# Batch 0's value products in one float32 part instead of three float32r parts

## The chip, the core and the metric

The kernel runs on one core of a Trainium2 chip. The core has a matrix engine (PE, with its weight loads listed as PEld), a vector engine (DVE), a scalar engine (ACT), a general engine (POOL) and a queue engine that sends DMAs (SP). The metric is device time in microseconds (us) from one execution; less is better.

## The reference

Three layers, one after the other, on 4 batches of 576 positions. The middle one is the place of the change.

```python
# 1. attention with a window of 32 (heads 0-3) or a dilated window (heads 4-7), 8 heads of 64
x = attn(q, k, v)                       # (4, 576, 512)
# 2. channel mix, w_r 512x512, w_k 512x1024, w_v 1024x512
xk = mu_k * x + (1 - mu_k) * x_prev
xr = mu_r * x + (1 - mu_r) * x_prev
k = np.maximum(xk @ w_k, 0.0)
v = k * k @ w_v
r = 1 / (1 + np.exp(-(xr @ w_r)))
x = r * v
# 3. gate to 2 of 4 experts, each a causal attention of width 64
```

## The kernel before

The work is laid out with features on partitions: a tile of activations is 128 features by 288 positions (half a batch, called a chunk, c = 0 or 1), and a product takes a 128x128 block of weights and streams the 288 columns past it. To come near float32 with the fast format float32r, `product` splits both factors in a rounded part and a rest (`hi`, `lo`) and adds three products of parts: hi by hi, hi weights by lo data, lo weights by hi data. So each pair of blocks costs three matmuls.

For the channel mix of a batch `b` (`dbatch`), PE makes per chunk `z` (4 outputs of `w_r`, function `receptance`), `h` (8 outputs of `w_k`, `keys`) and `v` (4 outputs of `w_v`, each over 8 blocks, `values_of`). Behind each `h` ACT takes the relu (`r`), then the square is halved and split in `kh` and `kl`; for batch 0 this is done with ACT and DVE passes over 128x288. Names such as `h_1_6` in the order below are chunk and output; `v_0_1` is chunk 0, output 1 of batch 0.

The weights come as 64-bit numbers. `load` brings a raw piece by DMA, `conv` makes float32 of it (`split_cols`: an ACT pass L679, two DVE passes L681 and L682) and splits it (ACT copy L687 to `w*_hi`, DVE subtraction L688 to `w*_lo`), each over 128x1024. The four pieces of `w_v` use the staging tiles `raw` and `vw` of the attention, and one in `x1`, so the first loads of batch 1's attention (`rqk`, L176, and `vw`, L204) wait until a piece is let go.

The attention of batch b+1 runs beside the channel mix of batch b. For a pair of heads (`sc_0` to `sc_3` are batch 1's pairs) q and k are loaded, turned by DVE (`qT`, `kT`; L276, for the dilated pairs 2 and 3 L271), PE makes scores (`sc`, L318), DVE masks them (L337), ACT takes exponents (L342), DVE scales (L354), PE turns the weights (`pt`, L382), ACT copies them (`pts`, L383), and PE multiplies by v (`av`, L394). A program-wide table of steps (`when`) says behind which step of `dbatch` a load or a `conv` is written, and the two streams are merged by `goal`. Within this a scheduler decides the order on each engine before the run; on the chip each engine then takes its instructions strictly in that order, so one that waits holds all behind it. The matmuls of attention are on plain float32 tiles.

Of the kernel before, what the change touches and what calls it, by code (L numbers as in the profile page):

```python
# [21 lines left out]
def tile_dilated_attention__rwkv_channel_mix__moe_attention(  # L22
# [131 lines left out]
    def load_qk(ap, dp, b, hp):  # L154

        dil = hp >= NP // 2
        qk = []
        if b == 0:  # L160
            if hp % 2 == 0:
                early["raw"] = dp.tile([128, 8, 512], F32R, tag=("wv_hi", "wv_lo")[hp // 2], name=f"rqk_{hp}",
                                       bufs=1).bitcast(F32).rearrange("p k f -> p (k f)")
# [343 lines left out]
    def mix_feature(n, c, w, f, b=0):  # L507

        t0 = CH * c
        x = X[b][:, f, 1 + t0 : 1 + t0 + CH]  # L510
        xp = X[b][:, f, t0 : t0 + CH]
        m, hi, lo = (a[:, f, :] for a in mixing[n])
        nc.scalar.activation(m, xp, AF.Copy, scale=mus[:, 1, w, f : f + 1])  # L513
        nc.vector.scalar_tensor_tensor(out=m, in0=x, scalar=mus[:, 0, w, f : f + 1], in1=m, op0=ALU.mult, op1=ALU.add)  # L514
        if b == 0:
            nc.scalar.copy(hi, m)
            nc.vector.tensor_sub(lo, m, hi.bitcast(F32))  # L517

# [45 lines left out]
    def keys(dp, b, c, fo, kh, kl, xk, wts):  # L564
# [10 lines left out]
        nc.vector.scalar_tensor_tensor(out=r, in0=r, scalar=0.5, in1=p if b else r, op0=ALU.mult, op1=ALU.mult)  # L575
# [11 lines left out]
    def dbatch(dp, dq, b, xr, wts, nxt):  # L587

        z, xk = [], []
        for c in range(2):  # L590
            z.append((dp if c else dq).tile([128, KT, CH], F32, tag=f"z{c}", name=f"z_{b}_{c}", bufs=1))
            for fo in range(KT):
                receptance(dp, b, c, fo, z[c], xr[c], wts)
# [3 lines left out]
        if b == 0:  # L597

            k2 = [(dp.tile(shape, F32R, tag="kh", name="kh_0_0", bufs=1), dp.tile(shape, F32R, tag="kl", name="kl_0_0", bufs=1)),
                  (xpool.tile(shape, F32R, tag="x3", name="kh_0_1", bufs=1), xpool.tile(shape, F32R, tag="x2", name="kl_0_1", bufs=1))]  # L600
# [13 lines left out]
        for c in range(2):  # L614
            k2 = (dp.tile(shape, F32R, tag="kh", name=f"kh_{b}_{c}", bufs=1), dp.tile(shape, F32R, tag="kl", name=f"kl_{b}_{c}", bufs=1))
            for fo in range(FT):
                keys(dp, b, c, fo, *k2, xk[c], wts)
# [3 lines left out]
            for fo in range(KT):  # L621
                values_of(b, c, fo, z[c], k2, wts)
# [38 lines left out]
    with tc.tile_pool(name="apool", bufs=2, side="left") as ap:  # L661
# [12 lines left out]
        def split_cols(raw, hi, lo, i):  # L674
# [7 lines left out]
            nc.vector.scalar_tensor_tensor(out=low, in0=high, scalar=3, in1=low,  # L682
                                           op0=ALU.logical_shift_left, op1=ALU.bitwise_or)
            w = low.bitcast(F32)
            cols = raw.shape[2]
            part_hi, part_lo = hi[:, :, i * cols : (i + 1) * cols], lo[:, :, i * cols : (i + 1) * cols]
            nc.scalar.copy(part_hi, w)  # L687
            marks["split"] = nc.vector.tensor_sub(part_lo, w, part_hi.bitcast(F32)).ins  # L688
# [4 lines left out]
        def load(x, i):  # L693
            pool, src, kts, cols = specs[x]
            if x not in wts:
                wts[x] = tuple(pool.tile([128, kts, cols], F32R, tag=f"w{x}_{h}", name=f"w{x}_{h}") for h in ("hi", "lo"))
            raws[x, i] = load_cols(src, kts, i, {"r": "hl", "k": "3RV1", "v": "RV1V"}[x][i])

        def conv(x, i):
            split_cols(raws.pop((x, i)), *wts[x], i)  # L700
            marks[f"split {x}{i}"] = marks["split"]


        when = {}
        for what, step in {"Lk1": 1, "r0": 18, "Lk2": 18, "r1": 22, "k0": 24, "Lk3": 24, "k1": 24, "Lv0": 24, "k2": 26,
# [20 lines left out]
        def mixed(b):  # L726
            yield from dbatch(dp, dq, b, mixes[b], wts, nxt(b))
# [8 lines left out]
        mixes[0] = [mixing[n][1:] for n in range(2)]  # L736
# [511 lines left out]
```

## Time and profile before

| | us |
|---|---|
| three runs | 548.56, 548.83, 549.34 |
| median | 548.83 |
| span of the profiled execution | 547.2 |

The profile is of one execution and shows its span, from the first to the last instruction; 1.6 us of the median lie around it. A row of a group of instructions has the line, the engine, the operation, its output and inputs by the program's names, shapes, the count, total busy us and mean ns of one, then the idle time ahead and what ended it. A matmul's record lasts longer than the distance to the next one, since matmuls are pipelined: its rate is read from the distance between starts.

### The profile page before, as it was taken

What the parts mean: (1) busy time and instruction counts of PE and PEld (TensorE: products, weight loads), DVE (VectorE), ACT (ScalarE), POOL (GpSimd) and SP (SyncE); (2) the same over time, 40 slices, a digit from 0 to 9 for tenths busy, and PEclk for the clock granted to TensorE, in tenths of its full rate; (3) what the DMA queues carried; (4) which work ended last, traced back from release to release, by engine and by line L of the source; (5) the groups of instructions that cost most, each with busy time, mean ns of one, the idle gap of its engine ahead of it and who ended that gap; (6) DMA issues with size and microseconds to landing.
All of it is one profiled execution on the core that took longest, in us unless ns stands there. A gap on an engine that the chain in (4) does not pass through costs nothing.

```text
span 547.2 us, 12500 instructions
## 1 busy us (share of the span) xinstructions
PE 525.8 (96%) x4653; PEld 476.1 (87%) x4657; DVE 350.8 (64%) x1153; ACT 336.4 (61%) x959; POOL 65.6 (12%) x99
## 2 busy tenths in 40 slices
PE   8987997999999999999999999999999999999996
PEld 4657996889999999999999999999977988988763
DVE  3788989695767588375451516448686559566752
ACT  2789978675884484663544526137576657656862
POOL 8500000010342031221022212000000000000000
PEclk9997999999999999999999999999999999999999
DMA  9959376876545663130100410055504705425313
GB/s 166 237 171 295 107 202 148 145 133 133 110 105 132 142 141 87 37 96 34 34 1 1 106 51 1 1 131 121 141 20 111 201 8 131 103 67 121 108 39 97
DMA packets 130173, 57.66 MB, mean 105 GB/s; under 512 B 109928, under 2 KB 117184, under 8 KB 130112
## 3 DMA queue, kind: packets, MB, share of 16 engines
q1 hardware_dynamic: 129392, 55.88, 43.2%
q8 instruction: 37, 0.61, 0.5%
q0 software_dynamic: 416, 0.44, 0.4%
q10 hardware_dynamic: 304, 0.53, 0.3%
q14 instruction: 24, 0.20, 0.1%
HBM read 34.42 MB, written 10.03 MB: 81 GB/s over the span
## 4 chain that ended last, share of the span: by engine, by line
PE 73%; DVE 9%; ACT 7%; SPq 4%; DMA 3%; issue 2%; POOL 1%; DVEq 0%; ACTq 0%; POOLq 0%
PE v L539 16%; PE h L539 11%; PE z L539 5%; PE av L1062 5%; PE pv L888 5%; PE po L1148 5%; PE pt L1025 4%; PE pq L539 4%; PE pk L539 4%; PE av L394 2%; PE sc L974 2%; PE sc L976 2%; SPq L189 2%; PE idle L76 2%; ACT pe L342 1%
## 5 line engine op out<-in xcount | busy, mean ns | idle before, releaser
L539 PE MATMUL h<-xh,wk_hi 128*128 128x288 f32 x256 | 76.3, 300 | 1.3 <-ACT r L568 0.8
L539 PE MATMUL v<-kh,wv_hi 128*128 128x288 f32 x256 | 74.9, 299 | 2.5 <-ACT r L568 1.9
L539 PE MATMUL h<-xl,wk_hi 128*128 128x288 f32 x256 | 75.5, 295 | 0.3 <-DVE xl L517 0.3
L539 PE MATMUL h<-xh,wk_lo 128*128 128x288 f32 x256 | 75.3, 294 | 0.4 <-DVE wk_lo L688 0.4
L539 PE MATMUL v<-kh,wv_lo 128*128 128x288 f32 x256 | 74.7, 296 | 0.0
L539 PE MATMUL v<-kl,wv_hi 128*128 128x288 f32 x256 | 74.7, 297 | 0.0
L986 ACT ACTIVATE pe<-pe,st 128x64 f32<-128x64 f32 (+4 forms) x80 | 44.8, 561 | 16.2 <-DVE st L980 15.8
L514 DVE SCALAR_TENSOR_TENSOR m<-x,mus,m 128x288 f32<-128x288 f32 x64 | 30.4, 512 | 34.5 <-ACT m L513 34.5
L529 POOL TENSOR_TENSOR xl<-m,xh 128x576 fp32r<-128x576 f32 x24 | 35.3, 1484 | 129.6 <-ACT xh L528 97.1
L539 PEld LDWEIGHTS v<-kh,wv_hi 128*128 128x128 f32 x256 | 47.6, 188 | 3.5 <-ACT r L568 2.3
L539 PEld LDWEIGHTS h<-xh,wk_hi 128*128 128x128 f32 x256 | 47.8, 187 | 2.7 <-ACT r L568 1.3
L539 PEld LDWEIGHTS h<-xh,wk_lo 128*128 128x128 f32 x256 | 48.2, 188 | 0.7 <-DVE wk_lo L688 0.7
L539 PEld LDWEIGHTS h<-xl,wk_hi 128*128 128x128 f32 x256 | 48.1, 188 | 0.5 <-DVE xl L517 0.5
L539 PEld LDWEIGHTS v<-kh,wv_lo 128*128 128x128 f32 x256 | 47.8, 188 | 0.4
L539 PEld LDWEIGHTS v<-kl,wv_hi 128*128 128x128 f32 x256 | 47.7, 188 | 0.4
L342 ACT ACTIVATE pe<-pe,st 128x96 f32<-128x96 f32 x108 | 39.0, 363 | 13.1 <-DVE st L337 13.1
L568 ACT ACTIVATE r<-h 128x288 f32<-128x288 f32 x64 | 25.8, 410 | 34.0 <-PE h L539 28.2
L980 DVE CUSTOM_DVE_ANT_0 pe<-sc,cmask 128x64 f32<-128x64 f32 (+4 forms) x80 | 33.1, 426 | 17.4 <-PE sc L976 17.0
L578 DVE TENSOR_TENSOR kl<-r,kh 128x288 fp32r<-128x288 f32 x50 | 31.1, 627 | 16.5 <-ACT kh L576 16.2
L539 PE MATMUL z<-xl,wr_hi 128*128 128x288 f32 x128 | 38.8, 304 | 0.1
L539 PE MATMUL z<-xh,wr_hi 128*128 128x288 f32 x128 | 38.8, 308 | 0.0
L539 PE MATMUL z<-xh,wr_lo 128*128 128x288 f32 x128 | 37.9, 299 | 0.0
(197 smaller groups left out, 1388.6 us busy)
## 6 DMA issues: line engine op xcount, KB each, us to landing
kk<-kh SPq DMA_DIRECT2D x32, 144.0 KB, 2.7
kl<-kl SPq DMA_DIRECT2D x32, 144.0 KB, 2.8
raw_in_moe_w_k_dram<-in_moe_w_k_dram SPq DMA_DIRECT2D x4, 1024.0 KB, 8.6
raw_in_moe_w_v_dram<-in_moe_w_v_dram SPq DMA_DIRECT2D x4, 1024.0 KB, 6.0
out_dram<-ob SPq DMA_DIRECT2D x14, 256.0 KB, 2.5
rqk<-in_q_dram SPq DMA_DIRECT2D x48, 72.0 KB, 2.6
rqk<-in_k_dram SPq DMA_DIRECT2D x48, 72.0 KB, 2.7
moved<-turned SPq DMA_DIRECT2D x8, 432.0 KB, 3.1
```

The source lines that it names most:

```text
L342: nc.scalar.activation(pe[:, t, :], pe[:, t, :] if b else sc[:, c0 : c0 + WK], AF.Exp, bias=st[:, 0, t : t + 1], scale=-1.0, accum_out=st[ ...
L514: nc.vector.scalar_tensor_tensor(out=m, in0=x, scalar=mus[:, 0, w, f : f + 1], in1=m, op0=ALU.mult, op1=ALU.add)
L529: nc.gpsimd.tensor_sub(lo[:, f], m[:, f], hi[:, f].bitcast(F32))
L539: marks["product"] = nc.tensor.matmul(o, w[:, kt, wsl], x[:, kt, :], start=(n == 0), stop=(n == last)).ins
L568: nc.scalar.activation(r, p, AF.Relu)
L578: half.tensor_sub(kl[:, fo, :], r, kh[:, fo, :].bitcast(F32))
L888: nc.tensor.matmul(p, x[:, kt, t0 : t0 + tn], w[:, kt, 512:772], start=(n == 0), stop=(n == 3 * KT - 1))
L980: nc.vector.tensor_tensor_reduce(out=pe[:tn, PO[t] + c0 : PO[t] + c1], in0=sc, in1=m, scale=-0.125, scalar=(BIG if i == 0 else st[:tn, 1, ...
L986: nc.scalar.activation(pb, pb, AF.Exp, bias=st[:tn, 0, t : t + 1], scale=-1.0, accum_out=st[:tn, 2, t : t + 1])
L1025: marks[f"turn {b}{e}"] = nc.tensor.transpose(pt[:kn, c0 : c0 + 128], pe[:, PO[t] + k0 : PO[t] + k0 + kn], ident).ins
L1062: ins = nc.tensor.matmul(av1[p0 : p0 + 64, q0 - 64 : q1 - 64], vh[kb][:kn], w[:kn, c0 : c0 + q1 - q0], start=(kb == blocks[0]), stop=(kb = ...
L1148: nc.tensor.matmul(sums[t], x[:, t0 : t0 + 128], w[:, h, :], start=(h == 0 and n == 0), stop=(h == 1 and n == 2))
```

## The change

The value products of batch 0, and no others, are made of whole float32 tiles: one matmul for each block of weights, with the halved square `k_0` as it is and the weights as they were put together. In detail:

- `conv` writes a piece of `w_v` out of its raw tile into a tile of its own (`wv_whole`, the fourth into `spare`); splitting it is a step of its own, `finish`, written at steps 66 to 72, after the value products of batch 0. `w_r` and `w_k` are finished in `conv`, as before, with their `lo` part in four tiles instead of one.
- In batch 0 `keys` writes one tile per chunk: for three outputs of four DVE multiplies the relu by the product in PSUM, and for every fourth ACT squares and halves it. There are no `kh` and `kl`.
- The first raw q and k of pairs 2 and 3 of batch 0 lie in the tile `wk_hi` instead of `wv_lo`.

```diff
     def keys(dp, b, c, fo, k2, xk):
         p = ps(bank(b), f"h_{b}_{c}_{fo}")[:, :CH]
-        product(p, wts["k"], xk, range(KT), slice(128 * fo, 128 * fo + 128))
+        weighted(p, b, "k", xk, fo)
         r = dp.tile([128, CH], F32, tag="r", name=f"r_{b}_{c}_{fo}", bufs=2)
         nc.scalar.activation(r, p, AF.Relu)
-        if b == 0 and 2 <= fo < 6:
-            nc.scalar.activation(r, r, AF.Square)
-            nc.scalar.activation(kh[:, fo, :], r, AF.Copy, scale=0.5)
-            nc.vector.scalar_tensor_tensor(out=kl[:, fo, :], in0=r, scalar=0.5, in1=kh[:, fo, :].bitcast(F32),
-                                           op0=ALU.mult, op1=ALU.subtract)
+        kh = k2[0]
+        if b == 0:
+            if fo % 4 == 3:
+                nc.scalar.activation(r, r, AF.Square)
+                nc.scalar.activation(kh[:, fo, :], r, AF.Copy, scale=0.5)
+            else:
+                nc.vector.scalar_tensor_tensor(out=kh[:, fo, :], in0=r, scalar=0.5, in1=p, op0=ALU.mult, op1=ALU.mult)
             return
...
+    def weighted(o, b, x, xs, fo):
+        cols = 1024 // (FT if x == "v" else KT)
+        i, at = divmod(128 * fo, cols)
+        wsl = slice(at, at + 128)
+        kts = range(KT if x != "v" else FT)
+        if b or x not in WHOLE:
+            product(o, (wts[x, "hi"][i], wts[x, "lo"][i]), xs, kts, wsl)
+            return
+        for kt in kts:
+            marks["product"] = nc.tensor.matmul(o, wts[x, "whole"][i][:, kt, wsl], xs[0][:, kt, :], start=(kt == 0),
+                                                stop=(kt == kts[-1])).ins
...
+        def finish(x, i):
...
+            nc.scalar.copy(hi, w)
+            marks[f"split {x}{i}"] = nc.vector.tensor_sub(lo, w, hi.bitcast(F32)).ins
+        WHOLE = "v"
```

The change moves instructions. On PE, the rows behind the scores of pair 1 are, before (`kh_0` and `kl_0` are the parts of chunk 0, `kh_1` and `kl_1` those of chunk 1):

```order
L382 MATMUL pt_0_0_1349<-ident,pe_0_1285 96x128 x3
L382 MATMUL pt_0_1_1380<-ident,pe_0_1285 96x128 x3
L539 MATMUL v_1_0_1624<-kl_1_1016,wv_hi 128x288
L539 MATMUL v_1_0_1624<-kh_1_1015,wv_lo 128x288
L539 MATMUL v_0_1_1703<-kh_0_1013,wv_hi 128x288
L539 MATMUL v_0_1_1703<-kl_0_1014,wv_hi 128x288
L539 MATMUL v_0_1_1703<-kh_0_1013,wv_lo 128x288
```

and in the changed kernel, from the first value product on:

```order
L557 MATMUL v_0_0_1487<-k_0_0_1015,wv_whole_1033 128x288 x8
L557 MATMUL v_1_0_1576<-k_0_1_1016,wv_whole_1033 128x288 x6
L318 MATMUL sc_1_5_1414<-kT_1_1409,qT_1_1407 64x96 x2
L318 MATMUL sc_1_0_1413<-kT_1_1409,qT_1_1407 64x96 x2
L318 MATMUL sc_1_5_1414<-kT_1_1409,qT_1_1407 64x96 x2
L318 MATMUL sc_1_0_1413<-kT_1_1409,qT_1_1407 64x96 x2
L382 MATMUL pt_0_0_1322<-ident,pe_0_1259 96x128 x3
L382 MATMUL pt_0_1_1351<-ident,pe_0_1259 96x128 x3
```

An output that took 24 rows takes 8, and the twelve of `h_1_7`, which stood ahead of `sc_0`, now stand between `sc_0` and `v_0_0`. Behind these rows stand four matmuls of `v_0_1`, the products `av_0_0`, a `pt`, the twelve of `h_1_6` and then the scores `sc_2`.

On DVE, where the last pieces of `w_k` and the first of `w_v` are converted (`raw_in_moe_w_k_dram_671` before and `_669` after is the piece for outputs 4 and 5), the rows before are:

```order
L688 TENSOR_TENSOR wk_lo<-raw_in_moe_w_k_dram_821,wk_hi 128x4x256
L517 TENSOR_TENSOR xl_1_3_996<-m_1_3_994,xh_1_3_995 128x288
L575 SCALAR_TENSOR_TENSOR r_0_1_1055<-r_0_1_1055 128x288
L688 TENSOR_TENSOR wk_lo<-raw_in_moe_w_k_dram_671,wk_hi 128x4x256
L517 TENSOR_TENSOR xl_1_3_996<-m_1_3_994,xh_1_3_995 128x288 x3
L578 TENSOR_TENSOR kl_0_1014<-r_0_0_1030,kh_0_1013 128x288
L681 TENSOR_SCALAR raw_in_moe_w_v_dram_845<-raw_in_moe_w_v_dram_845 128x1024
L578 TENSOR_TENSOR kl_0_1014<-r_0_1_1055,kh_0_1013 128x288
L682 SCALAR_TENSOR_TENSOR raw_in_moe_w_v_dram_845<-raw_in_moe_w_v_dram_845 128x1024
L572 SCALAR_TENSOR_TENSOR kl_0_1014<-r_0_2_1073,kh_0_1013 128x288
L575 SCALAR_TENSOR_TENSOR r_1_0_1091<-r_1_0_1091 128x288
L688 TENSOR_TENSOR wv_lo<-raw_in_moe_w_v_dram_845,wv_hi 128x8x128
```

and after:

```order
L748 TENSOR_TENSOR wk_lo_963<-raw_in_moe_w_k_dram_822,wk_hi 128x1024
L521 TENSOR_TENSOR xl_1_3_998<-m_1_3_996,xh_1_3_997 128x288
L593 SCALAR_TENSOR_TENSOR k_0_0_1015<-r_0_1_1052,h_0_1_1039 128x288
L701 TENSOR_SCALAR raw_in_moe_w_v_dram_845<-raw_in_moe_w_v_dram_845 128x1024
L748 TENSOR_TENSOR wk_lo_879<-raw_in_moe_w_k_dram_669,wk_hi 128x1024
L521 TENSOR_TENSOR xl_1_3_998<-m_1_3_996,xh_1_3_997 128x288 x3
L593 SCALAR_TENSOR_TENSOR k_0_0_1015<-r_0_2_1068,h_0_2_1055 128x288
L702 SCALAR_TENSOR_TENSOR wv_whole_1033<-raw_in_moe_w_v_dram_845 128x1024
L748 TENSOR_TENSOR wv_lo_1944<-wv_whole_1033,wv_hi 128x1024
L593 SCALAR_TENSOR_TENSOR k_0_1_1016<-r_1_0_1084,h_1_0_1071 128x288
```

The `kl` rows are gone, and the first pass over the first piece of `w_v` (L701) now stands ahead of the `wk_lo` of outputs 4 and 5. The split of that first piece still stands here although it is written at step 66; those of the other three pieces stand some 95, 130 and 160 rows further on, and the four copies to `wv_hi` stay in this stretch of ACT's order.

Also on DVE, the turning of pair 2's q (`qT_2`) stands before the change behind all the work on pair 1:

```order
L352 TENSOR_SCALAR st_1_1443<-st_1_1443 128x5
L353 RECIPROCAL st_1_1443<-st_1_1443 128x5
L354 TENSOR_TENSOR pe_1_1442<-pe_1_1442,st_1_1443 128x480
L271 STREAM_TRANSPOSE qT_2_1585<-rqk 128x144x4
L514 SCALAR_TENSOR_TENSOR m_0_4_1872<-x_1255,mus,m_0_4_1872 128x288
L271 STREAM_TRANSPOSE kT_2_1587<-rqk 128x144x4
```

and after it, ahead of the first look at pair 1's scores:

```order
L353 RECIPROCAL st_0_1260<-st_0_1260 128x5
L605 SCALAR_TENSOR_TENSOR x_212<-z_0_847,v_0_0_1487 128x288
L354 TENSOR_TENSOR pe_0_1259<-pe_0_1259,st_0_1260 128x480
L271 STREAM_TRANSPOSE qT_2_1537<-rqk 128x144x4
L337 ISA pe_1_1411,st_1_1412<-sc_1_5_1414,m_next 128x96
```

So `qT_2` moved ahead by the nine masked readings of `sc_1` and the scaling of `pe_1`.

## Rows read from the trace of the kernel before

**Rows 1.** The page: engines' shares of the chain that ended last.

```profile
PE 73%; DVE 9%; ACT 7%; SPq 4%; DMA 3%; issue 2%; POOL 1%; DVEq 0%; ACTq 0%; POOLq 0%
```

**Rows 2.** Stretches (from:to, length), busy us of PE, PEld, DVE, ACT, POOL; PE clock; DMA.

```profile
90.00:100.00 10.00, 7.82 (x84) 7.20 (x85) 9.97 (x55) 9.95 (x45) 0.00 (x0) 1.00 0.63 119
120.00:130.00 10.00, 10.00 (x129) 8.83 (x128) 7.89 (x36) 7.65 (x32) 0.00 (x0) 1.00 0.70 122
```

**Rows 3.** Waits of PE from 60 to 145 us: total us, times, longest.

```profile
PE v L539 <- ACT r L568: 1.9, 2, 1.2
PE sc L318 <- DVE kT L276: 0.9, 1, 0.9
PE h L539 <- ACT r L568: 0.8, 2, 0.5
PE sc L318 <- DVE kT L271: 0.7, 1, 0.7
PE pt L382 <- DVE pe L354: 0.7, 2, 0.5
PE h L539 <- DVE wk_lo L688: 0.4, 1, 0.4
PE h L539 <- DVE xl L517: 0.3, 1, 0.3
```

**Rows 4.** Timeline of PE around the first value product: start, duration, idle ahead.

```profile
87.37 0.29 PE L539 MATMUL h<-xh,wk_lo 128*128 128x288 f32 x1
87.81 1.06 PE L318 MATMUL sc<-kT,qT 64*64 64x96 f32 x36
90.04 0.40 PE L539 MATMUL v<-kh,wv_hi 128*128 128x288 f32 x1 [1.18 <-ACT r L568]
90.27 0.29 PE L539 MATMUL v<-kl,wv_hi 128*128 128x288 f32 x1
```

**Rows 5.** Pieces of the chain that ended last: start, length, what.

```profile
122.00 0.71 PE av L394 x20
...
275.02 12.77 PE v L539 x96
...
388.44 0.77 PE pt L1025 x7
```

**Rows 6.** Timeline of PEld in a float32 product of two experts, 512 then 384 columns.

```profile
400.57 0.20 PEld L1062 LDWEIGHTS av<-wt,vt 128*64 128x64 f32 x4
401.06 0.14 PEld L1062 LDWEIGHTS av<-wt,vt 128*64 128x64 f32 x2 [0.29 <-issue]
401.48 0.14 PEld L1062 LDWEIGHTS av<-wt,vt 128*64 128x64 f32 x2 [0.29 <-issue]
```

**Rows 7.** Groups of PE from 60 to 145 us: one of batch 0's three.

```profile
L539 PE MATMUL v<-kh,wv_hi 128*128 128x288 f32 x64 | 19.3, 304 | 1.9 <-ACT r L568 1.9
```

**Rows 8.** Groups of DVE from 58 to 142 us.

```profile
L688 DVE TENSOR_TENSOR wv_lo<-raw_in_moe_w_v_dram,wv_hi 128x1024 fp32r<-128x1024 f32 x4 | 4.9, 1224 | 1.5 <-ACT wv_hi L687 1.5
...
L578 DVE TENSOR_TENSOR kl<-r,kh 128x288 fp32r<-128x288 f32 x8 | 3.6, 455 | 0.1
L575 DVE SCALAR_TENSOR_TENSOR r<-r 128x288 f32<-128x288 f32 x8 | 3.5, 447 | 0.2
...
L681 DVE TENSOR_SCALAR raw_in_moe_w_v_dram<-raw_in_moe_w_v_dram 128x1024 uint32<-128x1024 uint32 x4 | 2.8, 690 | 0.0
```

**Rows 9.** Groups of ACT from 58 to 142 us.

```profile
L571 ACT ACTIVATE kh<-r 128x288 fp32r<-128x288 f32 x8 | 3.6, 448 | 0.1
L576 ACT CAST kh<-r 128x288 fp32r<-128x288 f32 x8 | 3.5, 447 | 2.1 <-DVE r L575 2.1
```

**Rows 10.** Timeline of SP's queue: the first load of batch 1's v.

```profile
95.94 0.44 SPq L204 DMA_DIRECT2D vw<-in_v_dram  x1
```

**Rows 11.** Timeline of DVE: turning pair 2's q and k.

```profile
105.21 1.17 DVE L271 STREAM_TRANSPOSE qT<-rqk 128x576 f32<-128x576 f32 x1 [3.73 <-DMA rqk<-in_q_dram]
...
107.28 1.16 DVE L271 STREAM_TRANSPOSE kT<-rqk 128x576 f32<-128x576 f32 x1 [0.61 <-DMA rqk<-in_k_dram]
```

More of the change, by code (lines that the diff above doesn't have):

```diff
@@ L161, in load_qk @@
             if hp % 2 == 0:
-                early["raw"] = dp.tile([128, 8, 512], F32R, tag=("wv_hi", "wv_lo")[hp // 2], name=f"rqk_{hp}",
+                early["raw"] = dp.tile([128, 8, 512], F32R, tag=("wv_hi", "wk_hi")[hp // 2], name=f"rqk_{hp}",
                                        bufs=1).bitcast(F32).rearrange("p k f -> p (k f)")
@@ L499, in begin_mix @@
         n = len(mixing)
+        if b == 0 and "rk"[n // 2] in WHOLE:
+            mixing[n] = ((dp if c else dq).tile(shape, F32, tag=f"xh{c}", name=f"x_{b}_{c}_{n}", bufs=1),)
+            return n
         mixing[n] = (mixing[0][0] if n == 1 else dq.tile(shape, F32, tag="m", name=f"m_{b}_{c}_{n}", bufs=1),
@@ L511, in mix_feature @@
         xp = X[b][:, f, t0 : t0 + CH]
-        m, hi, lo = (a[:, f, :] for a in mixing[n])
+        m = mixing[n][0][:, f, :]
         nc.scalar.activation(m, xp, AF.Copy, scale=mus[:, 1, w, f : f + 1])
         nc.vector.scalar_tensor_tensor(out=m, in0=x, scalar=mus[:, 0, w, f : f + 1], in1=m, op0=ALU.mult, op1=ALU.add)
-        if b == 0:
+        if b == 0 and len(mixing[n]) > 1:
+            hi, lo = (a[:, f, :] for a in mixing[n][1:])
             nc.scalar.copy(hi, m)
@@ L578, in keys, with values_of @@
         half.tensor_sub(kl[:, fo, :], r, kh[:, fo, :].bitcast(F32))
-    def values_of(b, c, fo, z, k2, wts):
+    def values_of(b, c, fo, z, k2):
         p = ps("mm", f"v_{b}_{c}_{fo}")[:, :CH]
-        product(p, wts["v"], k2, range(FT), slice(128 * fo, 128 * fo + 128))
+        weighted(p, b, "v", k2, fo)
         t0 = 1 + CH * c
@@ L597, in dbatch @@
         if b == 0:
[L599 to L600 removed]
+            k2 = [(dp.tile(shape, F32, tag="kh", name="k2_0_0", bufs=1),), (xpool.tile(shape, F32, tag="x3", name="k2_0_1", bufs=1),)]
             for fo in range(FT + 2):
@@ L681, in split_cols @@
             tc.keep_in_program_order(nc.vector.tensor_single_scalar(low, low, 29, op=ALU.logical_shift_right))
[L682 to L688, printed above, removed]
+            marks["split"] = nc.vector.scalar_tensor_tensor(out=w.bitcast(U32), in0=high, scalar=3, in1=low,
+                                                            op0=ALU.logical_shift_left, op1=ALU.bitwise_or).ins
         specs = {"r": (dq, w_r, 4, 512), "k": (dp, w_k, 4, 1024), "v": (dp, w_v, 8, 512)}
@@ L694, in load @@
             pool, src, kts, cols = specs[x]
-            if x not in wts:
-                wts[x] = tuple(pool.tile([128, kts, cols], F32R, tag=f"w{x}_{h}", name=f"w{x}_{h}") for h in ("hi", "lo"))
             raws[x, i] = load_cols(src, kts, i, {"r": "hl", "k": "3RV1", "v": "RV1V"}[x][i])
         def conv(x, i):
-            split_cols(raws.pop((x, i)), *wts[x], i)
-            marks[f"split {x}{i}"] = marks["split"]
+            pool, src, kts, cols = specs[x]
+            each = 1024 // kts
@@ new lines, in conv @@
+            parts = wts.setdefault((x, "whole"), [])
+            if x not in WHOLE:
+                raw = raws.pop((x, i))
+                w = raw[:, :, :, 0].bitcast(F32)
+                assemble(raw, w)
+                parts.append(w)
+                finish(x, i)
+                return
+            if i < cols // each - 1:
+                w = pool.tile([128, kts, each], F32, tag=f"w{x}_lo{i + 1}", name=f"w{x}_whole{i}", bufs=1)
+            elif x == "r":
+                w = dp.tile([128, kts, each], F32, tag="xl1", name=f"w{x}_whole{i}", bufs=1)
+            else:
+                if "spare" not in wts:
+                    wts["spare"] = dp.tile([128, 2, 1024], F32, tag="kl", name="spare", bufs=1)
+                w = wts["spare"][:, "kv".index(x)].rearrange("p (k c) -> p k c", k=kts)
@@ new lines, in conv @@
+            parts.append(w)
+            assemble(raws.pop((x, i)), w)
+            marks[f"split {x}{i}"] = marks["split"]
+        def finish(x, i):
+            pool, src, kts, cols = specs[x]
+            w = wts[x, "whole"][i]
+            if i == 0:
+                wts[x, "all"] = pool.tile([128, kts, cols], F32R, tag=f"w{x}_hi", name=f"w{x}_hi", bufs=1)
+                wts[x, "hi"], wts[x, "lo"] = [], []
+            each = 1024 // kts
+            hi = wts[x, "all"][:, :, i * each : (i + 1) * each]
+            lo = pool.tile([128, kts, each], F32R, tag=f"w{x}_lo{i}", name=f"w{x}_lo{i}", bufs=1)
+            wts[x, "hi"].append(hi)
+            wts[x, "lo"].append(lo)
+            nc.scalar.copy(hi, w)
+            marks[f"split {x}{i}"] = nc.vector.tensor_sub(lo, w, hi.bitcast(F32)).ins
@@ L711, in events @@
             for what in when.pop(n, []):
+                if what[0] == "F" and what[1] not in WHOLE:
+                    continue
                 if what[0] == "L":
@@ L715, in events @@
                         order_v()
+                elif what[0] == "F":
+                    finish(what[1], int(what[2]))
                 else:
@@ L726, in mixed @@
         def mixed(b):
-            yield from dbatch(dp, dq, b, mixes[b], wts, nxt(b))
+            yield from dbatch(dp, dq, b, mixes[b], nxt(b))
         first = attn_batch(ap, dp, dq, 0)
@@ L735, in tile_dilated_attention__rwkv_channel_mix__moe_attention @@
         run(first)
-        mixes[0] = [mixing[n][1:] for n in range(2)]
+        mixes[0] = [mixing[n][-2:] for n in range(2)]
         events(24)
```

34 lines of the change are left out of this document (18 added, 16 removed).

## The prediction

> **What bounds the kernel now.** I began with the chain of work that ended last: 73% of it lies on PE, DVE and ACT have 9% and 7% [rows 1]. So an edit counts by what it does to PE's busy time and to PE's waits, and the work of the other engines counts where PE waits for it. The stretches show that batch 0's channel mix, where the change acts, is the looser part: from 90 to 100 us PE is busy 7.82 us, DVE 9.97 and ACT 9.95; from 120 to 130 us PE is full again, and DVE has about 2 us free [rows 2]. PE's waits from 60 to 145 us, grouped by what ended them, sum to 5.7 us in ten waits, and more than half hang on work that the change takes away or lightens: the relus `r` that come late from ACT, the turned `kT` and the weights `pe` [rows 3].
>
> A wait costs more than its idle time. In the steady products of batch 1, 96 matmuls take 12.77 us, so 133 ns from start to start [rows 5], while a record lasts 0.29 us: a wait, counted from the record's end, leaves out some 0.16 us in which the next products would have run. Behind a wait the next start comes after 0.23 us (90.04 to 90.27) in place of 0.13 [rows 4], 0.10 more. So ten waits lose 5.7 + 10 x 0.26 = 8.3 us of PE. That is what can be gained by removing waits here, and no more.
>
> **The price of the products.** Batch 0 makes 8 outputs of 8 blocks, 64 products, and the trace has 64 matmuls for one of the three parts [rows 7]: 192 matmuls x 0.133 = 25.5 us. They become 64 float32 matmuls. The trace has none of 128x288, so I take the price per column from others. The ten `av` products of a half pair that the order lists stand as 20 records in the trace [rows 5]: a plain float32 product is two records. A record over 512 columns is spaced 0.42 us from the next (401.06 to 401.48) [rows 6], 0.82 ns a column; the next smaller case agrees, seven float32 transposes of 128 columns in 0.77 us, 0.86 ns a column [rows 5]. Against 0.133/288 = 0.46 ns for a float32r part, a record goes through its columns at about half the rate. So 288 columns cost about 0.242 us a record (0.84 ns a column, between the two), two records 0.484 us, and 64 products 31.0 us: **+5.5 us** of PE. One float32 product is dearer than the three float32r matmuls that it replaces (0.40 us).
>
> Does a weight load lie behind the columns? In [rows 6] the loads are spaced exactly as the columns ask, so they do; the weights there are 64 columns wide, and here 128. The transposes have 128 and show no load either, at half the length of a record that we will have. The first record of that group is spaced 0.49 from the one before, 0.065 us more than 0.42. I take 0; the upper bound is 0.065 on each of 128 records, 8.3 us. By the Trainium skill, *TensorE: Matmul & The Clock Gate*, "The mechanism", a weight load overlaps matmuls in flight only where the row group differs, and "LDWEIGHTS (loading the stationary operand)" gives 128 columns / 1.2 = 107 ns: an estimate of 13.7 us more for 128 records, some 564 us in all. By that rule float32 here would be plainly slower; the trace disagrees in [rows 5] and [rows 6], where no such gap stands between records.
>
> **What comes off DVE and ACT.** DVE loses 16 `kl` passes of about 0.45 us, and has 12 products of relu and PSUM in place of eight squarings: 7.2 - 1.8 = 5.4 us less. Three of four `wv_lo` of 1.22 us leave the stretch too, 3.7 us [rows 8]; they land after 105 us, where DVE has room (7.89 busy of 10) [rows 2], so I cost them there at nothing; with that cover gone they would be 3.7 us. ACT had 16 casts and copies to `kh` and eight squares; four of each remain: 16 passes of 0.45, 7.2 us less [rows 9]. The copies to `wv_hi` stay where they were.
>
> With this slack ACT keeps up with `r`: the waits of `h` (0.8) and `v` (1.9) for it go. The turning of pair 0's and 1's q and k no longer stands behind `kl` and `wv_lo`: `sc` for `kT` of L276 (0.9) goes, and so do `pt` for `pe` (0.7) and the 0.7 for L271 in their old form. Two stay: `h` for `wk_lo` (0.4) and for `xl` (0.3) lie ahead of anything that got lighter [rows 3]: with 0.26 each, 1.2 us. One grows: the first pass over the first piece of `w_v` (L701, as L681 before, 0.69 us [rows 8]) now stands ahead of the `wk_lo` of outputs 4 and 5, and PE waits for that split already. So 0.7 more: 1.9 us stay.
>
> **What is late next.** `qT_2` now stands ahead of the nine masked readings of `sc_1`, in an engine that takes its rows in order, and it waits for a load. Before, this row waited 3.73 us and started at 105.21, `kT_2` at 107.28 [rows 11], with nothing of pair 1 behind it. These loads follow the first load of batch 1's v, which went out at 95.94 [rows 10], when the fourth piece of `w_v` had been split in its staging tile. In the changed kernel the tile is free once `spare` is written (a pass of 1.22 us as L688's), behind three readings of `sc_0`. `sc_0` started at 87.81 [rows 4]; with the twelve products of `h_1_7` moved behind it (1.6 us) and the waits ahead changed by -1.3 and +0.7, it starts at about 85.6. One matmul group (1.06), three readings and the pass put the load at about 88.7, 7.2 us sooner. If q and k follow at the old distance, `qT_2` starts at 98.0 and k is there at 100.1.
>
> DVE then reads `sc_1` from 98.0 + 1.17 = 99.2 on, and turns k behind the readings, until about 102. PE reaches `sc_2` at about 101.4 (from 85.6: `sc_0` and `sc_1` 1.06 each, `h_1_7` and `h_1_6` 1.6 each, 18 value products 8.7, ten `av` 0.7, nine transposes 1.0: 15.7, and nothing that waits between). That is 0.5 of waiting at `sc_2`; `pe_1`, scaled last, makes `pt_1` wait about 1.3, and `av_1` 0.6: 2.4 us, an estimate. The bounds are 0 (the load may come sooner still, the row moved only ahead of idle time) and 3.73 (all of the old stall falls on PE).
>
> **Sum.** +5.5 for the products, -8.3 for the waits, +1.9 that stay, +2.4 new: +1.5 us. The profiled execution has a span of 547.2 and about 1.6 around it, 548.8, which is the median. So **550.3 us**. From 145 us on PE is near full, so I let the shift pass to the end unchanged. About 0.2% (1.1 us) is what a measurement of this kernel can tell from no change.
>
> **Rivals.**
> *The waits stay in another place (slower).* DVE was full to 9.97 of 10, PE's waits move to the loads and to the readings behind `qT_2`. For it: the order puts a waiting row ahead of pair 1. Against: 9 us of DVE and 7 of ACT go. At the full 8.3 us it gives 548.8 + 5.5 = 554.3; about 553 is its middle.
> *The waits go and none comes (faster).* The load comes as early as I say or 2.5 us sooner, and L701 is hidden because the piece of `w_v` is ready early. Then 1.2 of 8.3 stay: 5.5 - 7.1 = -1.6, **547.2 us**. It is faster from the point at which waits kept and new are under 1.7 us in all. For it: [rows 2] and [rows 3]; against: the 3.73 us that DVE waits for q in [rows 11].
> *The weight load shows.* 0.065 us on each of 128 records, and waits as forecast: about 558 us. The unwaited spacings of [rows 6] speak against it.
> *The product is cheaper.* If 288 columns passed in one record of 0.242 us, 64 would take 15.5: 10 us less than before, and with 4.3 of waits kept in place of 8.3 some 535 to 540. Against it: the 20 records of [rows 5]. By the Trainium skill, *Perfetto Trace Analysis*, "Engine Utilization", float32 runs at half the peak rate, an estimate of 15.4 us for 64 products; the trace disagrees, as two records at half rate each make a quarter.
>
> **Chances.** Forecast (549 to 551.6, waits of about 4 us) 0.46; waits stay 0.23; none comes 0.22; load shows 0.06; cheaper 0.03. The range takes the bounds of the first three: 547.0 to 554.3, leaving out the last two and a tail of the faster case. Faster than 547.7 holds most of "none comes" and "cheaper", 0.22; within 0.2% (547.7 to 549.9) the rest of it and the lower part of the forecast, 0.22; slower 0.56.
>
> **What would show it.** Right: `v` of batch 0 as 128 records of 128x288, 0.24 us apart in a row; no wait of `h` or `v` for `r` above 0.3 us; DVE idle ahead of `qT_2` for the load of q, and PE waiting at `sc_2` or `pt_1`; three `wv_lo` between 105 and 135 us; `z` of batch 1 starting 1 to 2 us later. Wrong: other spacing of the records (0.13 or 0.30), the load of v later than 90 us, waits of PE from 60 to 145 us under 1 us or above 5.

## The result and the profile after

The changed kernel takes 554.5 us (median of 4 runs, 553.6 to 555.1) against 549.1 for the kernel before (548.6 to 549.8): a ratio of 1.0096, with a 95% interval of 1.0081 to 1.0110. It is 5.4 us slower, where 1.5 was forecast with 554.3 as the range's end. The profiled execution has a span of 553.4 us, 6.2 more than before; it is the slowest of the four, 0.6 us above their median. Its chain by engine, to be held against [rows 1]:

```profile
PE 78%; DMA 6%; DVE 5%; ACT 5%; SPq 4%; issue 1%; POOL 0%; ACTq 0%; DVEq 0%
```

DVE and ACT, whose work shrank, have less of the chain; PE and DMA have more. The timeline of PE of the changed kernel, around the value products that answer to [rows 4] and [rows 5] (start, length, what, idle ahead):

```profile
88.07 6.95 PE L557 MATMUL v<-k,wv_whole 128*128 128x288 f32 x28
94.95 0.56 PE L318 MATMUL sc<-kT,qT 64*64 64x96 f32 x16
97.39 0.83 PE L382 MATMUL pt<-ident,pe 128*96 128x128 f32 x6 [1.88 <-DVE pe L354]
...
106.32 1.03 PE L318 MATMUL sc<-kT,qT 64*64 64x96 f32 x20 [2.54 <-DVE kT L271]
107.39 1.34 PE L394 MATMUL av<-pts,vw 96*64 96x32 f32 x20
109.12 0.84 PE L382 MATMUL pt<-ident,pe 128*96 128x128 f32 x3 [0.40 <-DVE pe L354]
...
117.80 0.80 PE L394 MATMUL av<-pts,vw 96*64 96x32 f32 x20
```

The price is as forecast: 28 records, 14 products, from 88.07 to 94.95 are 0.246 us each, so 128 records take 31.4 us against 25.5 for 192 matmuls at 0.133: +5.9 us (forecast 5.5). No weight load shows between records. The waits are not as forecast: 1.88 us ahead of pair 0's weights, and 2.54 ahead of `sc_2`. And behind the second one the same work takes longer: twenty `av` records last 1.34 us at 107.39 and 0.80 at 117.80. The stretches say why (length, busy of PE, PEld, DVE, ACT and POOL, then the granted clock, DMA share, GB/s):

```profile
100.00:104.00 4.00, 3.78 (x40) 3.01 (x38) 1.62 (x8) 0.28 (x1) 0.00 (x0) 1.00 0.59 94
104.00:108.00 4.00, 1.64 (x32) 1.38 (x34) 3.91 (x20) 4.00 (x21) 0.00 (x0) 0.82 0.84 136
108.00:112.00 4.00, 3.60 (x36) 2.33 (x33) 1.85 (x6) 2.85 (x8) 0.00 (x0) 0.50 0.84 156
112.00:116.00 4.00, 4.00 (x20) 2.85 (x20) 4.00 (x22) 3.33 (x18) 0.00 (x0) 0.83 0.17 39
```

The granted clock fell to 0.50, the lower level, 1.2 GHz. Four microseconds each at 0.82, 0.50 and 0.83 lack 0.72 + 2.0 + 0.68 = 3.4 us of full clock, and with 0.2 taken off for the 0.4 us in which PE waited anyway, 3.2 us of work. In the kernel before, the clock stayed at 1.00 throughout 60 to 145 us. Waits of PE in this stretch, which answer to [rows 3] (total us, times, longest):

```profile
PE sc L318 <- DVE kT L271: 2.5, 1, 2.5
PE pt L382 <- DVE pe L354: 2.3, 2, 1.9
PE h L544 <- DVE xl L521: 1.1, 1, 1.1
PE h L544 <- DVE wk_lo L748: 0.8, 1, 0.8
PE h L544 <- DVE k L593: 0.2, 1, 0.2
```

The reader is to see two things. All the waits that were to go are gone: none for `r`, none for the `kT` of L276. And the sum did not fall: 6.9 us in six waits, 8.5 with the 0.26 that a wait costs beside its idle time, against 8.3 before and 4.3 in the forecast. Where they come from stands in the queue of SP and on DVE of the changed kernel, against [rows 10] and [rows 11]:

```profile
82.34 0.43 SPq L690 DMA_DIRECT2D raw_in_moe_w_v_dram<-in_moe_w_v_dram  x1
...
93.09 0.44 SPq L204 DMA_DIRECT2D vw<-in_v_dram  x1
```

```profile
89.65 0.70 DVE L701 TENSOR_SCALAR raw_in_moe_w_v_dram<-raw_in_moe_w_v_dram 128x1024 uint32<-128x1024 uint32 x1 [2.91 <-DMA raw_in_moe_w_v_dram<-in_moe_w_v_dram]
90.26 0.77 DVE L276 STREAM_TRANSPOSE qT<-rqk 128x576 f32<-128x576 f32 x1
...
91.46 1.22 DVE L702 SCALAR_TENSOR_TENSOR spare<-raw_in_moe_w_v_dram 128x1024 uint32<-128x1024 uint32 x1
...
102.38 1.21 DVE L271 STREAM_TRANSPOSE qT<-rqk 128x576 f32<-128x576 f32 x1 [5.13 <-DMA rqk<-in_q_dram]
```

The fourth raw piece of `w_v` is issued at 82.34 and lands at 89.6; DVE stands at its first pass for 2.91 us, with `qT_1` and the readings of `sc_0` queued behind. `vw` is free after L702, so the load of v goes out at 93.09 and not at the forecast 88.7, pair 2's q follows it, and `qT_2` holds DVE for 5.13 us, with all readings of `sc_1` behind.

In all, batch 1's `z` starts at 145.4 us against 137.3, 8.1 later, and batch 2's 7.0 later. The first row of each view is where batch 0's `h` begins:

```profile
60.95 0.30 PE L539 MATMUL h<-xh,wk_hi 128*128 128x288 f32 x1
...
137.30 0.29 PE L539 MATMUL z<-xh,wr_hi 128*128 128x288 f32 x1
...
216.83 0.30 PE L539 MATMUL z<-xh,wr_hi 128*128 128x288 f32 x1
```

```profile
60.04 0.30 PE L544 MATMUL h<-xh,wk_hi 128*128 128x288 f32 x1
...
145.44 0.51 PE L544 MATMUL z<-xh,wr_hi 128*128 128x288 f32 x1
...
223.85 0.30 PE L544 MATMUL z<-xh,wr_hi 128*128 128x288 f32 x1
```

From batch 0's first `h` to batch 1's `z` PE has the same `h`, scores and attention products in both kernels, and takes 85.4 us in place of 76.35, 9.05 more; the changed kernel enters the stretch 0.9 us sooner. The terms give 5.9 + 0.2 + 3.2 = 9.3, so the stretch closes to 0.3. Between the two marks 1.1 us is given back: PE before waited 0.5 us once at an `h` of batch 1 for DVE's `r`, and after does not; with the restart that is 0.8, and 0.3 is not assigned. A further 0.8 is given back in the gate stage, where PE before waited 0.6 us for `ql` once, and after does not.

### The profile page after: what moved, and what is told of

Its sections match the earlier page's. It is cut to its first block, busy times and chain, and to the rows that moved or that the text cites. A ratio compares the mean times of both kernels' runs of the same rounds, so it can differ in the third digit from the quotient of the medians.

```text
span 553.4 us, 12354 instructions
## 1 busy us (share of the span) xinstructions
PE 532.9 (96%) x4593; PEld 475.6 (86%) x4593; DVE 345.9 (63%) x1141; ACT 331.1 (60%) x943; POOL 64.4 (12%) x99
## 4 chain that ended last, share of the span: by engine, by line
PE 78%; DMA 6%; DVE 5%; ACT 5%; SPq 4%; issue 1%; POOL 0%; ACTq 0%; DVEq 0%
PE v L544 14%; PE h L544 12%; PE z L544 7%; PE av L1113 5%; PE pv L939 5%; PE pt L1076 5%; PE pq L544 5%; PE pk L544 5%; PE po L1199 5%; PE v L557 4%; PE av L394 3%; PE sc L1025 3%; PE sc L1027 2%; DMA rqk<-in_q_dram 2%; PE sc L318 2%; SPq L189 2%
## 5 line engine op out<-in xcount | busy, mean ns | idle before, releaser
L544 PE MATMUL v<-kh,wv_hi 128*128 128x288 f32 x192 | 55.6, 298 | 0.6 <-DVE r L596 0.6
L544 PE MATMUL v<-kl,wv_hi 128*128 128x288 f32 x192 | 55.7, 296 | 0.0
L544 PE MATMUL v<-kh,wv_lo 128*128 128x288 f32 x192 | 55.7, 295 | 0.0
L599 DVE TENSOR_TENSOR kl<-r,kh 128x288 fp32r<-128x288 f32 x42 | 27.5, 658 | 16.3 <-ACT kh L597 16.2
L516 ACT ACTIVATE m<-x,mus 128x288 f32<-128x288 f32 x64 | 31.0, 533 | 9.9 <-POOL xl L534 6.7
L544 PEld LDWEIGHTS v<-kh,wv_hi 128*128 128x128 f32 x192 | 35.6, 188 | 1.2 <-DVE r L596 1.0
L544 PEld LDWEIGHTS v<-kh,wv_lo 128*128 128x128 f32 x192 | 35.9, 188 | 0.1
```

Of the source, the lines that this page charges most:

```text
L599: half.tensor_sub(kl[:, fo, :], r, kh[:, fo, :].bitcast(F32))
```

## The experiments

Ratios are to the kernel before, timed on the same chip, with their 95% intervals. A run that leaves out a part of the output says so in its expectation. Where a row of a run's profile is read, it is of one execution.

**The fourth piece staged elsewhere.**

```diff
-        stage = {..., "3": (xpool, "x3"), "R": (ap, "raw"), "V": (ap, "vw")}
+        stage = {..., "3": (xpool, "x3"), "2": (xpool, "x2"), "R": (ap, "raw"), "V": (ap, "vw")}
-            raws[x, i] = load_cols(src, kts, i, {"r": "hl", "k": "3RV1", "v": "RV1V"}[x][i])
+            raws[x, i] = load_cols(src, kts, i, {"r": "hl", "k": "3RV1", "v": "RV12"}[x][i])
```

> Changed kernel with one edit: the fourth raw piece of w_v is staged in tile x2, which is free there, and not in vw. Theory A (the rise is the price of the float32 products, 5.9 us, plus waits that moved to the readings of sc_0 and to qT_2, because both hang on the fourth piece of w_v: its raw load into vw lands at 89.6 us, DVE holds the readings of sc_0 behind its first pass, and vw comes free only after it): the waits of PE for pe (2.3) and for kT of L271 (2.5) fall under 1 us together, the load of batch 1's v goes out before 90 us, those for wk_lo and xl (1.9) stay; time 549 to 551. Theory B (the waits come from the longer value products or the order as such, wherever the piece is staged): PE still waits over 6 us from 60 to 145 us, 553.5 to 555.

Measured: 553.2 us, ratio 1.0074 (1.0061 to 1.0087). The load of v goes out at 89.1 us, the clock stays at 1.00, and the waits of PE from 60 to 147 us are these:

```profile
PE sc L318 <- DVE kT L271: 0.9, 1, 0.9
PE z L544 <- POOL xl L534: 0.8, 1, 0.8
PE h L544 <- DVE wk_lo L748: 0.8, 1, 0.8
PE h L544 <- DVE k L593: 0.6, 1, 0.6
PE h L544 <- DVE xl L521: 0.5, 1, 0.5
PE pt L382 <- DVE pe L354: 0.5, 1, 0.5
PE z L544 <- ACT xh L533: 0.4, 1, 0.4
PE av L394 <- ACT pts L383: 0.4, 1, 0.4
```

The two large waits went from 4.8 to 1.4 us, so the staging did set them; but the time fell by 1.3 us only, and by time theory B was nearer. New waits stand at `z` of batch 1, for the mixed x that needs batch 1's attention: what is gained ahead is partly lost there. In all the waits are 4.9 us in eight, 7.0 with restarts, against 8.5.

**The price alone, in the kernel before.**

```diff
-        product(p, wts["v"], k2, range(FT), slice(128 * fo, 128 * fo + 128))
+        if b == 0:
+            for kt in range(FT):
+                marks["product"] = nc.tensor.matmul(p, wts["v"][0][:, kt, 128 * fo : 128 * fo + 128].bitcast(F32),
+                                                    k2[0][:, kt, :].bitcast(F32), start=(kt == 0), stop=(kt == FT - 1)).ins
+        else:
+            product(p, wts["v"], k2, range(FT), slice(128 * fo, 128 * fo + 128))
```

> Kernel before with one edit: batch 0's value products are eight float32 matmuls on kh and the hi part of w_v (read as float32) in place of 24; the terms with kl and with the lo part are left out of the output, while the work that makes them stays. Theory A: the order on DVE is that of before, so the waits stay near 8 us less at most 1.5 that the longer products cover, and the price of 5.9 us shows nearly whole: 553.5 to 555. Theory B (the price is not what makes the changed kernel slow; most of it would lie beside waits): under 551.

Measured: 551.8 us, ratio 1.0054 (1.0042 to 1.0066). That is 2.8 us and between the theories. Sixteen records take 3.97 us (99.84 to 103.81), 0.248 each, so the price is there in full; about 3 of its 5.9 us are covered. PE's waits up to batch 1's `z` account for 1.5 of that (4.5 us in nine against 5.7 in ten), and the wait for `ql` in the gate stage, gone here too, for 0.8. The rows of the sixteen records:

```profile
99.84 4.05 PE L584 MATMUL v<-kh,wv_hi 128*128 128x288 f32 x16
103.81 0.39 PE L394 MATMUL av<-pts,vw 96*64 96x64 f32 x6
```

The waits for `kT` and `pe` of [rows 3] (2.3 us) are down to 0.3 here with all of DVE's work in place: a slower PE waits less for the others. So these waits, which the forecast credited to lighter DVE work, go with the dearer products alone; those for `r` do not (3.0 us here, 2.7 before).

**The exchange of waits alone.** The changed kernel with 52 of 64 products:

```diff
         kts = range(KT if x != "v" else FT)
+        if b == 0 and x == "v":
+            kts = range(7 - c)
...
-        weighted(p, b, "v", k2, fo)
+        weighted(p, b, "v", k2, fo, c)
```

> Changed kernel with one edit: of the 64 float32 value products of batch 0 only 52 are made (7 of 8 blocks for chunk 0, 6 for chunk 1; the others are left out of the output), so that at 0.491 us each they take 25.5 us of PE, what the three parts took before. All conversions, tiles and loads are those of the changed kernel. Theory A: only the exchange of waits is left, 9.9 us in place of 8.0 from 60 to 145 us and 0.8 less later: 549.5 to 551. If the waits did get fewer and a float32 product costs more than its spacing shows: under 548 for the first, over 552 for the second.

Measured: 550.9 us, ratio 1.0026 (1.0013 to 1.0040), as theory A had it: with the price taken out, what the change does to DVE, ACT and the loads is a loss of 1.9 us, not the gain of 4 that the forecast counted. The clock falls here too (0.50 from 108 to 112 us). The runs of this kernel spread from 547.8 to 551.9 us, and with the mean granted clock of each run: 547.8 at 0.994, 548.8 at 0.987, four from 549.1 to 550.5 at 0.985, six from 551.4 to 551.9 at 0.982 or 0.983. That is some 4 us between the run with the highest clock and those with the lowest. It is a correlation: some of the difference in clock may lie ahead of 60 us, and a longer wait may have come with the fall.

**Four edits to the order.** The conversion of the fourth piece later, in the table of steps:

```diff
-        "v2": 39, "v3": 42}
+        "v2": 39, "v3": 47}
```

> Changed kernel with one edit: the conversion of the fourth piece of w_v is written at step 47 in place of 42, so that DVE's two passes on it stand behind the scaling of pe_1 and ahead of qT_2. Theory A: the wait of pt_0 for pe_0 (2.0 with its restart) goes, but vw comes free later, so the load of batch 1's v and the q of pair 2 come later, and PE waits longer at sc_2 (over 3 us); in sum 552.5 to 555.5. Theory B (the first pass in front of the readings does not matter): the wait of pt_0 stays.

Measured: 556.4 us, ratio 1.0138 (1.0125 to 1.0151), slower than either theory said. The wait at `pt_0` went, as A had it; the wait at `sc_2` did not grow, against A. The load of v goes out at 103.3 us, the whole attention of batch 1 slips, and PE stands where it ends, 1.7 us for ACT's copy of x and 2.6 us at `z`, with the clock at 0.50 from 144 to 148 us.

Pair 2's q and k turned behind `pe_1`:

```diff
         later = tc.issue_after(marks["split v2"]) if (b, hp) == (1, 0) else ExitStack()
+        if (b, hp) == (1, 2):
+            later = ExitStack()
+            later.enter_context(tc.issue_after(marks["weights 0"]))
+            later.enter_context(tc.issue_after(marks["weights 5"]))
...
                            st[:, 2, t0:t1].unsqueeze(2).to_broadcast([128, n, WK])).ins
+            marks[f"weights {t0}"] = marks["first weights"]
```

> Changed kernel with one edit: the turning of pair 2's q and k on DVE is held behind the scaling of both halves of pe_1. Theory A (a row that waits for a load stands ahead of pair 1's readings and holds them): DVE reads sc_1 from about 97.5 us, the waits at pt_1 go, that at sc_2 falls from 2.5 to under 1 us, and TensorE's granted clock, which fell to 0.5 from 106.6 to 113.4 us behind these waits, stays at 1: 549 to 551.5. Theory B (the load of q is what PE waits for, wherever it stands, and the clock falls anyway): 553 to 555.

Measured: 550.5 us, ratio 1.0027 (1.0016 to 1.0037): theory A by time and by waits, with 4.1 of the 5.4 us back; the clock, though, did not stay at 1.00 in the profiled execution. `pe_1` is scaled at 100.6 and 102.4, and then the turning goes without a wait:

```profile
100.56 0.56 DVE L358 TENSOR_TENSOR pe<-pe,st 128x384 f32<-128x384 f32 x1
102.35 0.66 DVE L358 TENSOR_TENSOR pe<-pe,st 128x480 f32<-128x480 f32 x1
102.93 1.19 DVE L275 STREAM_TRANSPOSE qT<-rqk 128x576 f32<-128x576 f32 x1
104.11 1.17 DVE L275 STREAM_TRANSPOSE kT<-rqk 128x576 f32<-128x576 f32 x1
```

PE has three waits left from 60 to 160 us, 1.8 at `pt_0`, 0.7 for `wk_lo` and 0.6 for `xl`. A shorter fall of the clock stands behind that at `pt_0` in the profiled run (0.76 from 96 to 100, 0.81 from 100 to 104 us), which is the slowest of twelve.

The same with the fourth piece in x2, and the passes over the first piece behind the `wk_lo` of outputs 4 and 5:

```diff
-            assemble(raws.pop((x, i)), w)
+            with tc.issue_after(marks["split k2"]) if i == 0 else ExitStack():
+                assemble(raws.pop((x, i)), w)
```

> Changed kernel with three edits: the fourth raw piece of w_v staged in x2 (as in the first experiment), pair 2's q and k turned behind pe_1, and the first pass over the first piece of w_v held behind the wk_lo of outputs 4 and 5. Theory A (each of these waits is its own and can be taken away by itself): the waits at pt_1, sc_2 and av_1 (2.3 us with restarts in the first experiment) and 0.6 of the wait for wk_lo go: 549.5 to 551.5. Theory B (waits go to whatever is next): 552.5 to 554.

Measured: 550.4 us, ratio 1.0023 (1.0012 to 1.0034), inside A's range, but no better than the turning alone. In the profiled execution, the slowest of twelve, the waits taken away came back as 1.4 us for pair 0's `kT` and 1.5 at `z` for the mixed x.

The turning behind `pe_1`, and the fourth piece converted between `pe_0` and the readings of `sc_1`:

```diff
-        "v2": 39, "v3": 42}
+        "v2": 39, "v3": 45}
```

> Changed kernel with two edits: pair 2's q and k turned behind pe_1 (as before), and the conversion of the fourth piece of w_v written at step 45 in place of 42, which puts DVE's two passes on it behind the readings of sc_0 and the scaling of pe_0 and ahead of the readings of sc_1. Theory A (both rows that wait for a load held pair 0 and pair 1; vw comes free hardly later, since the piece lands only at 89.6 us): the waits at pt_0 and sc_2 are both gone or under 0.7 us, no half clock from 80 to 130 us, and against the run with the turning alone 0 to 2 us are gained: 548.5 to 550.5. Theory B (what is gained at pt_0 is lost where batch 1's attention ends, since its loads come later: waits of z for the mixed x): 550.5 to 553.

Measured: 553.3 us, ratio 1.0062 (1.0048 to 1.0076), theory B by time. The waits at `pt_0` and `sc_2` shrank (0.4 and 0.9 us), no half clock shows behind 60 us, and the load of v went out at 97.1 us, not "hardly later"; `z` waits 1.5 us. It is 2.9 us behind the run with the turning alone by the medians, 1.9 by the ratios. Its waits are more: seven of 5.1 us against three of 3.1, so 3.0 with restarts, among them those at `z` and 0.5 at an `av` for the load of v.

**Filling the wait.** Three idle products ahead of `sc_2`:

```diff
+            if (b, hp) == (1, 2):
+                p = ps("mm", "fill")
+                for _ in range(3):
+                    nc.tensor.matmul(p[:, :480], qT[:, :128], qT[:, :480], start=True, stop=True)
```

> Changed kernel with one addition: three float32 matmuls of 128 by 480 columns on pair 2's turned q, whose result nobody reads, between h_1_6 and sc_2 on PE, so that most of the wait for kT_2 is filled with work. Theory A (the clock fell because PE stood still there, and the 6.8 us at half clock cost about 3.4 us): no stretch at 0.5 between 100 and 120 us, and although PE does 2.4 us more, 550.5 to 552.5. Theory B (the fall of the clock has nothing to do with this wait, or costs nothing): 554 to 556.

Measured: 556.6 us, ratio 1.0142 (1.0125 to 1.0158). By time theory B; but the experiment is confounded. PE's order changed, `sc_1` now waits 1.45 us and `pt_0` 1.75, and the clock falls behind those, ahead of the fill:

```profile
92.00:96.00 4.00, 1.06 (x36) 0.90 (x36) 3.24 (x15) 2.63 (x13) 0.00 (x0) 1.00 0.88 184
96.00:100.00 4.00, 3.36 (x30) 2.41 (x30) 2.46 (x21) 3.84 (x19) 0.00 (x0) 0.56 1.00 163
100.00:104.00 4.00, 4.00 (x17) 3.57 (x16) 2.07 (x4) 1.64 (x7) 0.00 (x0) 0.58 0.58 97
```

So it shows another fall of the clock behind PE's idleness, and not what filling would be worth.

**What lighter DVE work is worth by itself.** In the kernel before, first with the `kl` subtractions of outputs 0, 1, 6 and 7 on POOL:

```diff
-        half = nc.gpsimd if b == 1 and fo % 2 == 0 and fo < FT - 2 else nc.vector
+        half = nc.gpsimd if b == 1 and fo % 2 == 0 and fo < FT - 2 or b == 0 else nc.vector
```

> Kernel before with one edit: the eight kl subtractions of outputs 0, 1, 6 and 7 of batch 0 run on POOL, which stands idle there, and not on DVE. Theory A (DVE's work is what PE waits for in batch 0's channel mix, so lighter DVE without a dearer product is a gain): DVE has 3.6 us less, waits of PE from 60 to 145 us fall by 1 to 3 us: 546 to 548. Theory B (the waits hang on ACT and on loads, or POOL is too slow): 548.5 to 550.

Measured: 552.1 us, ratio 1.0056 (1.0044 to 1.0068), theory B. POOL's eight passes last 1.4 us each on average, the first two 5.65 together, where DVE takes 0.455 for one [rows 8]; so the two `r` tiles go late, ACT waits 3.68 us for that, and PE for ACT (5.0 us in two waits), with 0.50 of clock from 72 to 76 us. A miss as a test of DVE's load, since it made something else late.

Then with all `kl` passes left out:

```diff
-            nc.vector.scalar_tensor_tensor(out=kl[:, fo, :], in0=r, scalar=0.5, in1=kh[:, fo, :].bitcast(F32),
-                                           op0=ALU.mult, op1=ALU.subtract)
             return
...
+        if b == 0:
+            return
         half = nc.gpsimd if b == 1 and fo % 2 == 0 and fo < FT - 2 else nc.vector
...
+            for _, kl in k2:
+                nc.gpsimd.memset(kl.bitcast(F32), 0.0)
```

> Kernel before with one edit: batch 0's 16 kl passes on DVE (7.2 us) are left out, and POOL sets both kl tiles to zero ahead of the channel mix, so that the value products read zeros for kl (the lo part of the squares is left out of the output); the 24 matmuls of an output, the splits of the weights and the loads stay. Theory A (lighter DVE work does not take PE's waits away: rows that wait for the pieces of w_v move ahead of the splits and readings that PE needs, as L681 of the first piece does here ahead of wk_lo and L681 of the fourth ahead of the readings of sc_0): PE waits 6 to 10 us from 60 to 145 us, 547.5 to 550. Theory B (the slack alone is worth the waits, as the forecast had it): under 4 us of waits, 543 to 546.

Measured: 547.4 us, ratio 0.9969 (0.9958 to 0.9981). This is faster, by 1.8 us: less than theory B's 3 to 6, and with 4.9 us of waits left, fewer than A's 6 to 10; the time is 0.1 below A's range. Most of the waits that are left are new ones:

```profile
PE sc L318 <- DVE st L352: 1.7, 1, 1.7
PE av L394 <- ACT pts L383: 1.4, 2, 1.1
PE h L539 <- DVE xl L517: 0.8, 1, 0.8
PE v L539 <- ACT kh L574: 0.6, 1, 0.6
```

In this kernel too the first pass over the first piece of `w_v` stands ahead of a `wk_lo`, but PE does not wait for it. The first pass over the fourth stands ahead of the readings of `sc_0`, as it does in the kernel before; there it showed no wait, and here, where DVE comes to it sooner, it waits 0.83 us for its load. `qT_2` stays behind pair 1's work, so lighter DVE work alone did not pull that row ahead.

**The turning and the equal price together**, by the two diffs above:

> Changed kernel with two edits from earlier experiments together: 52 of the 64 float32 value products (the other 12 are left out of the output), which take the 25.5 us that the three parts took, and pair 2's q and k turned behind pe_1. Theory A (three separate terms: the price 5.9, the row that waits for q 4, the rest a gain on the kernel before): 550.45 less 3 to 5.9: 544.5 to 547.5. Theory B (with shorter products the waits that the price now covers come back): 548 to 550.

Measured: 551.8 us, ratio 1.0056 (1.0040 to 1.0072): slower than the same kernel with 5.9 us more of products (550.5), and above both theories. Theory A's sum of separate terms falls here: with the shorter products the turning gains nothing (550.9 without it). The profile, of the slowest of six executions (554.3), has 2.6 us of waiting at `z` for ACT's `xh`, behind batch 1's attention, and 0.50 of clock there from 144 to 148 us. That PE's waits come back at the end of the stretch because batch 1's attention and mix end when their loads, DVE and ACT let them is how I read it; no edit shows it.

## Why the prediction was wrong

The mechanism that was forecast is there, row by row; its size was not, and a second one was missed. What came is nearest to the first rival, the waits that stay in another place: 554.3 us. Two of the signs of being wrong came as well, the load of v later than 90 us (93.09) and waits above 5 (6.9).

The price was right: 5.5 forecast, 5.9 from the spacing, with two records to a product and no weight load between them. The rule of the Trainium skill (*TensorE: Matmul & The Clock Gate*, "The mechanism") that would have put a load between records is not borne out here at 0.246 us a record. Nor does a product run at half the rate, as I had read the figure in *Perfetto Trace Analysis*, "Engine Utilization", of the Trainium skill (for FP32_LOW_HIGH): one record does, and a product has two.

The removal was right as to which waits go. The two that were to stay, for `wk_lo` and `xl`, did, at 1.9 us of idle and 2.4 with their restarts (1.9 forecast).

The step that failed is "What is late next", and in it the term of 2.4 us for new waits. Measured, they are 5.0 us of idle (2.5, 2.3 and 0.2), 6.0 with restarts. It was mis-sized first since I let the load of v go out at 88.7 us on the assumption that the fourth piece of `w_v` is there when DVE comes to it. DVE came 2.91 us before it was: the issue stands at its old place in SP's queue (82.34 us; 81.90 before), and lands 7.3 us later. In the kernel before this pass showed no wait, as DVE was busy until 89.40:

```profile
89.40 0.68 DVE L681 TENSOR_SCALAR raw_in_moe_w_v_dram<-raw_in_moe_w_v_dram 128x1024 uint32<-128x1024 uint32 x1
```

So lighter work of DVE ran into a transfer that had been hidden, which held the readings of `sc_0` (a wait not forecast) and put `qT_2` at 102.4 in place of 98.0. Of the single edits to the changed kernel, moving that row pair gives the most back: 4.1 us, the fall of the clock included. But this gain holds beside the dearer products only, as the run with both edits shows.

The assumption is not all that was wrong in this step. With the fourth piece in x2 the load of v goes out at 89.1 us, and `qT_2` starts here, close to the forecast 98.0:

```profile
97.30 1.15 DVE L271 STREAM_TRANSPOSE qT<-rqk 128x576 f32<-128x576 f32 x1 [2.56 <-DMA rqk<-in_q_dram]
```

Yet that run takes 553.2 us. Its new waits are 3.6 us in six, 5.2 with restarts, among them 1.2 at `z`, where the end of batch 1's attention holds PE; the forecast had no term for that, as it let the shift pass on from there.

What was missed altogether is TensorE's clock. Behind the wait at `sc_2` it fell to the lower level, 3.4 us of full clock lost. Of the price of a wait I had counted only its idle time and its restart. In the profiled execution the stretch from batch 0's `h` to batch 1's `z` closes with this term and lacks 3 us without it. What it costs in the time of the kernel is not shown by an edit. The runs of the kernel with 52 products agree in size, but are a correlation; the attempt to fill the wait failed; and in the run with the fourth piece in x2 the fall is gone, with 1.5 us of waits, while the time is only 1.3 us lower. Without the clock, the forecast's own sum with measured terms is 5.9 - 8.3 + 8.5 = +6.1, near the measured 5.4. It comes so near since the clock's 3.2 us and the 2.8 that were won elsewhere (0.9 ahead of the stretch, 1.1 and 0.8 behind it) about cancel, which is luck.

The sum, too, was built wrongly in one respect. It added the price to the waits as if they were independent. Alone, the price is 2.8 us and not 5.9, and leaving out the `kl` passes alone brings 1.8 us. These two and the 4.1 for the row that waits make 5.1 of the measured 5.4. This closing is of three separate kernels, each with an order of its own, and the run with both the turning and the cheaper products shows that such terms need not add up.

## What to carry to other kernels

Where a busy engine is made lighter, look at each transfer that lands while it was busy: it showed no wait before, and may be the next one. A row that waits for a load, moved ahead by a scheduler in an engine that takes its rows in order, can cost more than the work that was saved. Where two engines wait for each other, a dearer product and the waits beside it are not a sum: time each alone, and then both together.

## What the runs showed of the hardware

A plain float32 matmul of 128x128 by 288 columns goes as two records of 0.246 us, so 0.49 us, against 0.40 for three float32r matmuls: for one product of this size splitting in three parts is the cheaper on PE. And a wait on PE can cost more than its length: in the profiled runs of eight of the thirteen kernels here the granted clock fell to 0.50 behind 60 us for some microseconds, each time at or just behind waits of PE, from one of 4.4 us for `r` down to two of 0.8 and 0.7 at `z`. The kernel before, with single waits up to 1.2 us, kept 1.00, as did four others, one of them with a wait of 1.7 us; the length of the last wait alone does not tell them apart.
